# A quarter of the side turns of block 0 go to batch 2, and the last weights are queued behind the evictions

## The chip, the cores and the metric

The kernel runs on one core of one Trainium2 chip. A core has a matrix engine (TensorE, PE in the profile), a vector engine (VectorE, DVE), an activation engine (ScalarE, ACT), a general engine (GpSimd, POOL) and SyncE (SP), which here issues all transfers. Each has its own instruction queue and works through it in order; semaphores tie them together. The metric is the device time of one execution in microseconds.

## The reference

Three networks in a row, on 8 batches of 576 tokens, 512 channels:

```python
# 1 attention: softmax of q over channels, of k over tokens
kv = einsum('bhsd,bhse->bhde', k_s, v);  x = einsum('bhsd,bhde->bhse', q_s, kv)
# 2 Fourier mixing and an MLP
u  = x + real(fft(fft(x, axis=1), axis=2))
un = (u - mean(u)) / sqrt(var(u) + 1e-6)
x  = u + maximum(un @ w_ch1, 0) @ w_ch2            # 512 -> 2048 -> 512
# 3 channel mixing with the token before
xk = mu_k * x + (1 - mu_k) * x_prev;  xr = mu_r * x + (1 - mu_r) * x_prev
k  = maximum(xk @ w_k, 0)                          # 512 -> 1024
out = sigmoid(xr @ w_r) * ((k * k) @ w_v)
```

## The kernel before

The 4608 tokens are cut into nine blocks of 512 (`blocks`, 0 to 8), which don't coincide with the eight batches (0 to 7): block 1 holds tokens of batches 0 and 1, block 2 of 1 and 2, and so on. Each float32 product is made of three float16 products (high by high, high by low, low by high), so that every weight has to be split into two float16 halves on the chip first.

**The main loop** (lines 966 to 1023) is network 2's MLP, block by block. For each of 16 column groups f, `mm1(f)` issues 12 matmuls into a PSUM bank `h` (two buffers), which ACT (`hh`, line 988) and DVE (`hl`, line 989) evict into two float16 halves; this pair is called the eviction here. `mm2(f - 2)` issues 12 matmuls that add the halves of two groups before into four banks `acc`. At the end of a block, line 1021 adds `acc` to `U` on DVE and line 1022 stores it.

**The strands** run beside it. `front_x` is attention, batch after batch, each in two halves (`attention`, lines 318 to 435: a maximum and exponentials of k and q on DVE and ACT, the product `kv`, three groups of transposes, four products into `U`). `front_y` is the Fourier transform of a batch (`transform`) and, for each block whose last batch is done, its normalisation (`norm`); block i + 1 can start only when `norm(i + 1)` and `halves(i + 1)` are done. `front_z` decodes and splits the MLP's weights during block 0. All three are Python generators. Their PSUM tiles in block 0 and later are `side0` and `side1`, one buffer each, taken by turns in the order in which the program asks for them (`aside`, line 64).

`side()` (line 935) gives the strands their turns: it is called 3 times in `mm1(f)` for f below 8 of block 0, twice in any other `mm1`, twice in each `mm2`. While block 0 runs, a call makes eight steps, x and y by turns, until attention of batch 1 is done; then four steps of y alone until `norm(1)` is done (line 939); then x, y, x, y.

**The last strand** (`last_strand`, line 951) gets one step in each call of `side()` once the three fronts are done. Its steps are: 1 of set-up; 40 pieces that take the largest absolute value of network 3's weights (lines 716 and 717); two that turn it into scales; 40 pieces that decode (lines 165 to 168) and 40 that split (lines 755 and 756), by turns; then `load_y(0)`, which reads block 0 back, `bound(0)` (lines 776 to 794), `mix(0, 1)` and `mix(0, 0)` (lines 798 to 828), which make the inputs of network 3 for block 0. If they are not used up when block 8 ends, the loop at line 1024 calls `side()` until they are.

**Network 3** (lines 1028 to 1098): for each block four groups of 12 matmuls with `wr` (line 1046), then eight of `mmk` (line 1059) and eight of `mmv` (line 1074). Line 1046 of block 0 reads what `mix(0, 1)` made, line 1059 what `mix(0, 0)` made.

The order in each engine's queue isn't the program's. A scheduler at build time runs through the program with a timeline of its own, and puts next on each engine the earliest traced instruction that is ready then, so a piece of a strand can stand far ahead of its place in the program. Where an order is wanted, `mark(name, ...)` remembers instructions, and `with behind(name):` lets every instruction traced under it on the same engine come after them (lines 308 to 316).

Of the kernel before, what the change touches and what calls it, by code (L numbers as in the profile page):

```python
# [13 lines left out]
AF = mybir.ActivationFunctionType  # L14
ALU = mybir.AluOpType
# [28 lines left out]
def net(ctx, tc, q, k, v, w1, w2, mu_k, mu_r, w_k, w_v, w_r, ce_d, se_d, cs_d, ss_d, alt_d, id_d, out):  # L44
    nc = tc.nc
# [13 lines left out]
    def bank(tag, bufs, shape=(128, 512)):  # L59
        return ps.tile(list(shape), F32, tag=tag, name=tag, bufs=bufs)  # L60
# [17 lines left out]
    def segments(i):  # L78

        t0, n = blocks[i]  # L80
        done, found = 0, []
        while done < n:
            b, s = divmod(t0 + done, S)
            m = min(n - done, S - s)
            found.append((b, s, m, done))
            done += m
        return found
# [179 lines left out]
    def w1t(t, f):  # L267

        k = place[0, 4 * (f // 4) + t]
        o = 128 * (f % 4)  # L270
        return wf[:, k, o:o + 128], wf[:, k, 512 + o:640 + o]

    def w2t(f, x):
        k = place[1, f]
        o = 128 * x
        return wf[:, k, o:o + 128], wf[:, k, 512 + o:640 + o]
# [31 lines left out]
    def mark(name, *ins):  # L308
        marks[name] = ins

    def behind(name):

        es = ExitStack()
        for i in marks.get(name, ()):
            es.enter_context(tc.issue_after(i.ins))
        return es
# [127 lines left out]
    done_att = [-1]  # L444
# [115 lines left out]
    done_norm = [-1]  # L560
# [115 lines left out]
    def halves(i):  # L676

        halves_part(i, 0, blocks[i][1])
# [178 lines left out]
    def front_x():  # L857
        for b in range(B):
            yield from attention(b)
        front_left[0] -= 1  # L860

    def front_y():
        for b in range(B):
            yield from transform(b)
            for i in range(NB):
                if segments(i)[-1][0] == b:
                    yield from norm(i)
        front_left[0] -= 1

    def front_z():  # L870
        for c in range(17):
            if c < 16:
                decoded(0, c)
            if c > 0:
                squares(0, c - 1)
            yield 0
        scales(0)
        for c in range(16):
            largest(c)
            yield 0  # L880
        scales(1)
        for c in range(4):
            split(0, c)
            yield 0
        for c in range(4):
            decoded(1, c)
            yield 0
        for c in range(2):
            split(1, c)
            yield 0  # L890
        started[0] = True
        have[:] = 4, 2
        for c in range(2, NF):
            if c + 2 < NF:
                decoded(1, c + 2)
            split(1, c)
            have[1] += 1
            yield 0
            if c < NF - 2:
                split(0, c + 2)  # L900
                have[0] += (c + 2) % 4 // 3 * 4
            yield 0
        front_left[0] -= 1
        stage.close()
        W["fx"] = front.enter_context(tc.tile_pool(name="fx", bufs=1))
# [4 lines left out]
    def run(g):  # L910
        for _ in g:
            pass

    def step(g):

        return next(g, None)

    nc.scalar.preload_act_table_set("natural_log_exp_and_others")
    sx, sy, sz = front_x(), front_y(), front_z()
# [13 lines left out]
    late = [None]  # L933

    def side():

        if done_block[0] < 0:

            turns = (sx, sy) * 4 if done_att[0] < 1 else (sy,) * 4 if done_norm[0] < 1 else (sx, sy) * 2
        else:  # L940
            turns = (sx, sy) * (2 if done_block[0] < 3 else 1)
        for g in turns:
            with behind(BEHIND_X.get(half[0]) if g is sx else None):
                step(g)
        if front_left[0] == 0:
            if late[0] is None:
                front.close()
                late[0] = last_strand()
            step(late[0])

    def last_strand():
        yield from last_weights()
        while done_block[0] < NB - 2:
            yield -1
        load_y(0)
        yield 0
        yield from mix(0, 1)
        yield from mix(0, 0)
        if NB > 1:
            load_y(1)  # L960
        late_done[0] = True
# [4 lines left out]
    for i, (t0, n) in enumerate(blocks):  # L966
        acc = [bank(f"acc{x}", 1) for x in range(4)]
        H = {}

        def mm1(f):  # L970
            if i == 0:

                while have[0] < min(f + AHEAD, NF):
                    assert step(sz) is not None
            xh, xl = un[i]
            pt = bank("h", 2)

            m = 256 if i == 0 and f < 8 else n
            for o in range(0, n, m):
                for t in range(4):  # L980
                    wh, wl = w1t(t, f)
                    for z, (a, c) in enumerate(((wh, xh), (wh, xl), (wl, xh))):
                        mm(out=pt[:, o:o + m], lhsT=a, rhs=c[:, t, o:o + m], start=(t == z == 0), stop=(t == 3 and z == 2))  # L983
                    if t == 1:
                        side()
            hh = hq.tile([128, 512], F16, tag="hh", name="hh", bufs=3)
            hl = hq.tile([128, 512], F16, tag="hl", name="hl", bufs=3)
            nc.scalar.activation(out=hh[:, 0:n], in_=pt[:, 0:n], func=AF.Relu)  # L988
            nc.vector.scalar_tensor_tensor(out=hl[:, 0:n], in0=pt[:, 0:n], scalar=0.0, in1=hh[:, 0:n], op0=ALU.max, op1=ALU.subtract)  # L989
            H[f] = hh, hl  # L990
            side()

        def mm2(f):
            if i == 0:
                while have[1] < min(f + AHEAD, NF):
                    assert step(sz) is not None
                if f == NF - LAG:
                    run(sz)
            hh, hl = H.pop(f)
            for x in range(4):  # L1000
                wh, wl = w2t(f, x)
                for z, (a, c) in enumerate(((wh, hh), (wh, hl), (wl, hh))):
                    mm(out=acc[x][:, 0:n], lhsT=a, rhs=c[:, 0:n], start=(f == z == 0), stop=(f == NF - 1 and z == 2))  # L1003
                if x == 1:
                    side()
            side()

        for f in range(NF):
            mm1(f)
            if f >= LAG:  # L1010
                mm2(f - LAG)
        if i + 1 < NB:
            while done_norm[0] < i + 1:
                side()
            halves(i + 1)
        for f in range(NF - LAG, NF):
            mm2(f)
        for x in range(4):
            for b, s, m, o in segments(i):
                y = U[b][:, x, s:s + m]  # L1020
                nc.vector.scalar_tensor_tensor(out=y, in0=acc[x][:, o:o + m], scalar=wsc[:, 6:7], in1=y, op0=ALU.mult, op1=ALU.add)
                nc.sync.dma_start(out=yT[x, :, t0 + o:t0 + o + m], in_=y)
        done_block[0] = i
# [10 lines left out]
    for i, (t0, n) in enumerate(blocks):  # L1034
# [7 lines left out]
        for x, (o, m) in enumerate(subs):  # L1042
            pt = bank("h", 2)
# [167 lines left out]
```

## Time and profile before

| | us |
|---|---|
| median of three runs | 1581.63 (1581.33 to 1582.81) |
| profiled execution | 1582.21 |
| its span in the profile | 1580.4 |
| PE busy in the span | 1465.5 (93%) |
| DVE busy | 938.1 (59%) |
| ACT busy | 652.0 (41%) |
| POOL busy | 245.0 (16%) |

The stages on the span's clock: attention and transform of batch 0 until 103, block 0 from 106 to 247, block 1 from 259.75, block 2 from 382.04, block 3 from 508.84, block 7 from 927.4 to 1021, block 8 from 1021.7 to 1104.8, network 3 from 1104.83. A busy PE isn't idle, but it can run at the lower of two clocks; the granted clock of a stretch (1.00 is 2.4 GHz, 0.50 is 1.2 GHz) tells. Idle time of an engine other than PE costs nothing by itself.

### The profile page before, as it was taken

Reading aid. Unit: us, or ns where it says so; the run is one execution under the profiler, and the core shown is the slowest. Engines: PE = TensorE matmul, PEld = TensorE weight load, DVE = VectorE, ACT = ScalarE, POOL = GpSimd, SP = SyncE. Lnnn points to the kernel's source line nnn. Section 1 sums busy time; section 2 is a strip of 40 time slices with the busy share of each in tenths; the row PEclk is TensorE's granted clock in tenths of the full one; section 3 lists DMA queues with packets and bytes.
Section 4 is the critical chain, followed back from the end, with each engine's and each line's share of the span. In section 5 each row is a group of like instructions: output and inputs, shape, how many; then the busy total and the mean of one; then the engine's idle time right before and its main releaser. Section 6 shows DMA issues by size and latency. Waiting matters only on the chain.

```text
span 1580.4 us, 18510 instructions
## 1 busy us (share of the span) xinstructions
PE 1465.5 (93%) x7135; PEld 765.2 (48%) x7135; DVE 938.1 (59%) x1646; ACT 652.0 (41%) x1167; POOL 245.0 (16%) x183
## 2 busy tenths in 40 slices
PE   5547998997998999999999998999999999999999
PEld 4434654554554555555555443444444444444444
DVE  7789726647658665474452778551785456554423
ACT  5675523423334332333321555241665445544322
POOL 1525522002002020010100236200000000000000
PEclk8769998998998999999999999999999999999999
DMA  8665103202112101101001834100111011100000
GB/s 308 211 205 177 48 1 103 64 1 74 48 47 74 48 33 43 48 32 42 1 7 47 288 117 145 40 26 14 67 54 51 4 54 54 54 0 27 27 27 27
DMA packets 46292, 108.20 MB, mean 68 GB/s; under 512 B 5979, under 2 KB 12412, under 8 KB 46204
## 3 DMA queue, kind: packets, MB, share of 16 engines
q1 hardware_dynamic: 46204, 107.02, 19.8%
q8 instruction: 56, 0.92, 0.2%
q14 instruction: 32, 0.26, 0.1%
HBM read 88.12 MB, written 18.87 MB: 68 GB/s over the span
## 4 chain that ended last, share of the span: by engine, by line
PE 71%; DVE 16%; ACT 4%; DMA 3%; issue 2%; POOL 2%; SPq 0%; POOLq 0%; ACTq 0%; DVEq 0%
PE h L983 18%; PE acc L1003 18%; PE h L1059 12%; PE acc L1074 9%; PE h L1046 4%; PE side L508 2%; PE side L528 2%; PE side L376 1%; DVE aa L820 1%; PE side L429 1%; DMA raw<-in_w_dram 1%; DVE wr L215 1%; DVE eo L463 1%; DVE d L657 1%; DVE wr L214 1%
## 5 line engine op out<-in xcount | busy, mean ns | idle before, releaser
L983 PE MATMUL h<-unh,wr 128*128 128x512 f16 (+1 forms) x1216 | 378.7, 375 | 23.3 <-DVE hl L989 14.0
L1003 PE MATMUL acc<-hh,wr 128*128 128x512 f16 x1152 | 367.6, 380 | 3.2 <-ACT wr L264 2.0
L983 PEld LDWEIGHTS <-wr 128*128 128x128 f16 x1824 | 177.3, 99 | 224.4 <-issue 36.9
L1003 PEld LDWEIGHTS <-wr 128*128 128x128 f16 x1728 | 165.2, 98 | 194.8 <-issue 5.9
L983 PE MATMUL h<-unl,wr 128*128 128x512 f16 (+1 forms) x608 | 226.6, 373 | 4.5 <-DVE unl L671 4.5
L1003 PE MATMUL acc<-hl,wr 128*128 128x512 f16 x576 | 219.6, 381 | 0.0
L989 DVE SCALAR_TENSOR_TENSOR hl<-h,hh 128x512 f16<-128x512 f32 x144 | 99.0, 688 | 187.0 <-ACT hh L988 186.2
L1074 PE MATMUL acc<-wvh,kke 128*128 128x512 f16 x576 | 181.3, 379 | 0.0
L1059 PE MATMUL h<-x,wkh 128*128 128x512 f16 x576 | 171.3, 379 | 0.0
L988 ACT ACTIVATE hh<-h 128x512 f16<-128x512 f32 x144 | 85.1, 592 | 187.8 <-PE h L983 187.4
L1074 PEld LDWEIGHTS <-kke 128*128 128x128 f16 x864 | 84.5, 98 | 102.0
L1064 ACT ACTIVATE kke<-kke 128x512 f32<-128x512 f32 x72 | 45.1, 626 | 166.7 <-DVE kke L1063 163.0
L1063 DVE SCALAR_TENSOR_TENSOR kke<-h,rg 128x512 f32<-128x512 f32 x72 | 49.6, 689 | 102.6 <-PE h L1059 102.3
L1074 PE MATMUL acc<-wvl,kke 128*128 128x512 f16 x288 | 109.2, 379 | 0.0
L1059 PE MATMUL h<-x,wkl 128*128 128x512 f16 x288 | 109.1, 379 | 0.0
L1046 PE MATMUL h<-wrh,x 128*128 128x512 f16 x288 | 88.6, 379 | 1.5 <-ACT kke L1047 1.5
L1059 PEld LDWEIGHTS <-wkh 128*128 128x128 f16 x576 | 55.7, 98 | 65.8
L1066 DVE TENSOR_TENSOR kke<-kke 128x512 f16<-128x512 f32 x72 | 49.7, 690 | 60.7 <-ACT kke L1065 60.3
L1046 PEld LDWEIGHTS <-x 128*128 128x128 f16 x432 | 42.3, 98 | 53.3 <-issue 3.0
L605 POOL TENSOR_TENSOR sq<-u 128x128 f32<-128x128 f32 (+7 forms) x15 | 23.8, 1588 | 281.4 <-DVE u L550 142.7
L826 POOL TENSOR_TENSOR s<-s 128x1024 f32<-128x1024 f32 x9 | 21.2, 2351 | 284.6 <-ACT s L824 234.2
L820 DVE SCALAR_TENSOR_TENSOR aa<-y,ms,aa 128x512 f32<-128x512 f32 x72 | 61.8, 866 | 5.0 <-ACT aa L816 3.0
(335 smaller groups left out, 2232.5 us busy)
## 6 DMA issues: line engine op xcount, KB each, us to landing
raw<-in_w_dram SPq DMA_DIRECT2D x24, 512.0 KB, 4.4
words<-in_w_dram SPq DMA_DIRECT2D x24, 512.0 KB, 4.3
vt<-in_v_dram SPq DMA_DIRECT2D x16, 650.0 KB, 5.1
kt<-in_k_dram SPq DMA_DIRECT2D x16, 576.0 KB, 3.9
qt<-in_q_dram SPq DMA_DIRECT2D x16, 576.0 KB, 3.7
out_dram<-oo SPq DMA_DIRECT2D x36, 256.0 KB, 2.1
y<-yT SPq DMA_DIRECT2D x8, 1026.0 KB, 4.9
raw<-in_w_k_dram SPq DMA_DIRECT2D x32, 256.0 KB, 3.9
```

Of the source, the lines that this page charges most:

```text
L508: mm(out=pt, lhsT=a[:, e, g, js], rhs=c[:, g, :], start=first, stop=(e == 1 and g == 1 and a is el))
L820: nc.vector.scalar_tensor_tensor(out=a, in0=y[:, t, 1:n + 1], scalar=mu[:, w, 0, t:t + 1], in1=a, op0=ALU.mult, op1=ALU.add)
L983: mm(out=pt[:, o:o + m], lhsT=a, rhs=c[:, t, o:o + m], start=(t == z == 0), stop=(t == 3 and z == 2))
L988: nc.scalar.activation(out=hh[:, 0:n], in_=pt[:, 0:n], func=AF.Relu)
L989: nc.vector.scalar_tensor_tensor(out=hl[:, 0:n], in0=pt[:, 0:n], scalar=0.0, in1=hh[:, 0:n], op0=ALU.max, op1=ALU.subtract)
L1003: mm(out=acc[x][:, 0:n], lhsT=a, rhs=c[:, 0:n], start=(f == z == 0), stop=(f == NF - 1 and z == 2))
L1046: mm(out=pt[0:m, :], lhsT=a[:, t, o:o + m], rhs=c[:, t, :], start=(t == 0 and a is rh and c is wrh), stop=(t == 3 and a is rl))
L1059: mm(out=pt[:, 0:n], lhsT=a[:, t, fs], rhs=c[:, t, 0:n], start=(t == 0 and a is wkh and c is kh), stop=(t == 3 and a is wkl))
L1063: nc.vector.scalar_tensor_tensor(out=kr[:, 0:n], in0=pt[:, 0:n], scalar=0.0, in1=G[:, 0:n], op0=ALU.max, op1=ALU.mult)
L1064: nc.scalar.activation(out=kr[:, 0:n], in_=kr[:, 0:n], func=AF.Square, scale=2.0 ** -76)
L1066: nc.vector.tensor_tensor(out=l2[:, 0:n], in0=kr[:, 0:n], in1=h2[:, 0:n], op=ALU.subtract)
L1074: mm(out=acc[x][0:m, :], lhsT=a[:, o:o + m], rhs=c[:, f, :], start=(f == 0 and a is h2 and c is wvh), stop=(f == NFK - 1 and a is l2))
```

## The change

Of the four steps in a call of `side()` in block 0, between the end of batch 1's attention and the end of `norm(1)`, the third goes to x. And each step of the last strand is traced behind the latest eviction that was traced before it: its ACT instructions after that `hh`, its DVE instructions after that `hl`. PE, POOL and SP instructions of the step are not held.

```diff
@@ side()
-            turns = (sx, sy) * 4 if done_att[0] < 1 else (sy,) * 4 if done_norm[0] < 1 else (sx, sy) * 2
+            turns = (sx, sy) * 4 if done_att[0] < 1 else (sy, sy, sx, sy) if done_norm[0] < 1 else (sx, sy) * 2
@@
             if late[0] is None:
                 front.close()
                 late[0] = last_strand()
-            step(late[0])
+            with behind("out"):
+                step(late[0])
@@ mm1(f)
-            nc.scalar.activation(out=hh[:, 0:n], in_=pt[:, 0:n], func=AF.Relu)
-            nc.vector.scalar_tensor_tensor(out=hl[:, 0:n], in0=pt[:, 0:n], scalar=0.0, in1=hh[:, 0:n], op0=ALU.max, op1=ALU.subtract)
+            ma = nc.scalar.activation(out=hh[:, 0:n], in_=pt[:, 0:n], func=AF.Relu)
+            mv = nc.vector.scalar_tensor_tensor(out=hl[:, 0:n], in0=pt[:, 0:n], scalar=0.0, in1=hh[:, 0:n], op0=ALU.max, op1=ALU.subtract)
+            mark("out", ma, mv)
             H[f] = hh, hl
             side()
```

## Rows read from the trace of the kernel before

**Rows 1.** Busy time by stretch: from:to, length, five engines (instructions), granted clock, DMA share, GB/s

```profile
247.00:262.00 15.00, 8.23 (x24) 4.51 (x23) 9.59 (x15) 7.25 (x13) 5.38 (x3) 0.66 0.43 141
360.00:390.00 30.00, 21.22 (x98) 11.40 (x97) 22.46 (x36) 10.48 (x16) 9.03 (x6) 0.83 0.29 97
490.00:515.00 25.00, 17.75 (x70) 10.84 (x69) 24.80 (x38) 10.73 (x20) 3.87 (x3) 0.73 0.27 98
...
927.00:1021.50 94.50, 86.86 (x390) 38.60 (x389) 69.69 (x157) 43.75 (x93) 42.47 (x38) 0.98 0.28 89
1021.50:1104.80 83.30, 83.30 (x388) 37.95 (x387) 29.50 (x59) 22.73 (x37) 2.34 (x1) 1.00 0.07 26
909.60:913.50 3.90, 3.83 (x10) 1.37 (x10) 3.87 (x17) 3.69 (x10) 0.74 (x1) 0.56 0.75 254
```

**Rows 2.** PE's waits, 880 to 924, then 955 to 1002: sum, times, longest

```profile
PE h L983 <- DVE hl L989: 3.8, 2, 3.0
...
PE h L983 <- DVE hl L989: 7.6, 5, 2.7
```

**Rows 3.** Timeline in block 7: start, length, engine, line, operation [idle before, releaser]

```profile
977.81 0.57 ACT L988 ACTIVATE hh<-h 128x512 f16<-128x512 f32 x1
...
978.37 0.95 DVE L756 SCALAR_TENSOR_TENSOR wvl<-dec,pw,wvh 128x256 f16<-128x256 f32 x1
...
979.58 0.68 DVE L989 SCALAR_TENSOR_TENSOR hl<-h,hh 128x512 f16<-128x512 f32 x1
...
980.31 0.38 PE L983 MATMUL h<-unh,wr 128*128 128x512 f16 x1 [2.74 <-DVE hl L989]
```

**Rows 4.** Groups by line: pieces of the last strand on DVE (busy us, mean ns)

```profile
L756 DVE SCALAR_TENSOR_TENSOR wvl<-dec,pw,wvh 128x256 f16<-128x256 f32 x16 | 8.8, 564 | 3.5 <-ACT wvh L755 3.5
...
L167 DVE SCALAR_TENSOR_TENSOR dec<-raw,dec 128x256 uint32<-128x256 uint32 x40 | 16.9, 433 | 0.0
...
L166 DVE TENSOR_SCALAR dec<-raw 128x256 uint32<-128x256 uint32 x40 | 15.1, 377 | 0.1
```

**Rows 5.** Timeline: bound and mix of block 0, last eviction, start of network 3

```profile
869.34 2.26 DVE L781 TENSOR_REDUCE z<-y 128x1 f32<-128x2052 f32 x1
...
1027.33 0.29 DVE L689 TENSOR_REDUCE z<-side 128x1 f32<-128x128 f32 x1 [1.49 <-PE side L688]
...
1029.23 1.33 ACT L816 ACTIVATE aa<-y,ms 128x512 f32<-128x512 f32 x2 [1.53 <-DVE ms L791]
...
1038.67 0.68 DVE L822 TENSOR_TENSOR x<-aa,x 128x512 f16<-128x512 f32 x1
...
1097.89 0.69 DVE L989 SCALAR_TENSOR_TENSOR hl<-h,hh 128x512 f16<-128x512 f32 x1 [4.49 <-ACT hh L988]
1103.30 2.73 DVE L1021 SCALAR_TENSOR_TENSOR u<-acc,wsc,u 128x512 f32<-128x512 f32 x4 [4.72 <-PE acc L1003]
...
1104.83 0.38 PE L1046 MATMUL h<-wrh,x 128*128 128x512 f16 x1
...
1115.73 0.59 PE L1059 MATMUL h<-x,wkh 128*128 128x512 f16 x2
```

**Rows 6.** Timeline: side banks in block 0, then the starts of blocks 1 and 2

```profile
196.26 0.47 PE L508 MATMUL side<-seh,eh 128*128 128x256 f32 x1
...
202.85 0.47 PE L508 MATMUL side<-seh,eh 128*128 128x256 f32 x1
...
244.20 1.06 PE L376 MATMUL side<-vt,kt 128*128 128x130 f32 x8
...
250.70 1.89 DVE L336 TENSOR_REDUCE m<-kt 128x256 f32<-128x1024 f32 x1 [0.69 <-DMA kt<-in_k_dram]
...
259.75 1.06 PE L983 MATMUL h<-unh,wr 128*128 128x512 f16 x2
...
269.50 1.16 PE L376 MATMUL side<-vt,kt 128*128 128x130 f32 x8
...
382.04 1.01 PE L983 MATMUL h<-unh,wr 128*128 128x512 f16 x2 [0.30 <-ACT unh L670]
```

## The prediction

> **What bounds the kernel now.** I read the engine shares first: PE is busy 93% of the span, so only its idle time and its time at the lower clock can be won. Then busy time by stretch, to see where these lie, since a share over the whole span hides it. Three places belong to the first edit: the ends of blocks 0, 1 and 2, where PE idles 6.8, 8.8 and 7.3 us and the granted clock of the stretch is 0.66, 0.83 and 0.73 [rows 1]. One belongs to the second: blocks 6 and 7, where PE's list of waits has seven on `hl`, 3.8 and 7.6 us in sum [rows 2]. Block 8, beside which DVE is busy 29.5 of 83.3 us, loses nothing [rows 1]: it is the cover that the second edit has to use.
>
> Third, the timeline at one such wait [rows 3]. `mm1` starts at 980.31, 0.05 us after the `hl` of the group just before it ends (979.58 + 0.68). So although `h` has two buffers, the schedule takes again the one freed last, and the next `mm1` waits for the newest eviction. Its cover is one `mm2`, 12 matmuls or 2.6 us. `hh` (0.57) and `hl` (0.68) fit in that if they go at once, with some 1.3 us to spare; here a split piece of 0.95 us and a decode stand between them [rows 3].
>
> **Second edit, what it wins.** The pieces were moved by the scheduler to before the evictions that precede them in the program. Held behind, at most the four pieces of one group stand between two evictions. By the groups by line a split costs DVE 0.56 us, a decode 0.38 + 0.43 [rows 4]; two of each, which is the program's rate, make 2.7 us, with `hl` 3.4, in a group of 5.2 us (83.3 / 16 in block 8 [rows 1]). They can start as soon as `hl` is done, so the next eviction finds its queue empty. Won: 3.8 + 7.6 = 11.4 us of waiting, and the clock that dropped after two of the waits: the stretch behind the 3.0 us wait runs at 0.56 for 3.9 us with PE busy, which loses 1.7, twice 3.4 [rows 1, 2]. Together 14.8 us. I keep 1.0 back for stray waits: 13.8. Lower bound: only block 6 is cleared, since no piece can run in it any more (3.8 + 1.7 = 5.5); upper 14.8.
>
> **Second edit, what it costs.** Every step of the last strand is held, not only the weights. Count the turns. `norm(8)` waits for `halves(7)` at the end of block 6; four of its 11 steps fit in the four calls left there, so the fronts end in the eighth call of block 7, and the strand gets 57 of that block's 64 calls. Block 8 gives 64 more: 121. But the weights take 1 + 40 + 2 + 80 = 123 steps. So two splits, `load_y(0)`, `bound(0)`, `mix(0, 1)` and `mix(0, 0)` are traced after block 8, behind its last eviction. Now they run far ahead: the reduction of `bound(0)` at 869.34, the mixes from 1029.23, `mix(0, 1)` done at 1039.35 [rows 5], hidden by block 8. After the change none of it starts before that eviction ends at 1098.58, and the first matmul of network 3, at 1104.83 now, needs it [rows 5]. The transfer of `load_y(0)` goes by SP and isn't held. Queued behind the held instructions is nothing but network 3 itself; the `acc` additions at 1103.30 (2.73 us for four) are ready in the midst and go first [rows 5].
>
> DVE's queue from 1098.58: the pieces of the last seven calls and the two after them, six splits and three decodes, 6 x 0.56 + 3 x 0.81 = 5.8; the additions 2.73; the reduction 2.26 [rows 4, 5]. That is 1109.4. Then the maximum over partitions through PE and the small scales: from 1027.33 to 1029.23, less an `hl` of 0.69 that ran in it, 1.2 [rows 5]; with the product before them, some 2: 1111.4. Four tiles of `mix(0, 1)`: from 1029.23 to 1039.35 is 10.1, less the reduction of another block (2.26) and two `hl` (1.4): 6.5 [rows 5]. So the last tile is there at 1117.9. The four tiles arrive 1.6 us apart and the first of the four `wr` groups takes them as they come, so it ends at 1118 where it now ends at 1107.4 (a group takes 2.6 us; the four fill the time from 1104.83 to 1115.73, bar 0.5 of smaller products [rows 5]): 10.6 us late. The next three groups, 7.8 us, cover `mix(0, 0)`, so that little is added there. PE stands idle for several us before it: after the idle time at the ends of blocks 0 to 2 the clock was granted at its lower level for part of the stretch [rows 1], so I add 1 us. Cost 11.6. Bounds: if the pieces are done while PE is still in block 8, the chain is the PE product at 1104.83 itself (everything of block 8 goes first on PE, which is why the present one waits until 1027), + 2 + 6.5, so 1113.3 and 6 us late; if the additions, splits and both mixes lie one behind the other with a slow stretch, 17. I take 11.6, near the middle, since it is the sum of the queue.
>
> Second edit: -13.8 + 11.6 = **-2.2** us (from -8.8 to +11.5).
>
> **A rule that speaks against this.** The waits repeat at each group. The Trainium skill, Perfetto Trace Analysis, section Optimization Strategy, says that the same gap repeating on the engine that should be saturated can mean that PSUM is too short for the next tile. By it the bank, not the queue, would be the cause, and the waits of block 7 would come again with any pieces beside it; the sum would be -5.5 + 11.6 = +6.1. The rows bear out the half of it, that the newest bank is waited for.
>
> **First edit.** Batch 2's first half now asks for its banks after all 13 of batch 1's transform and norm: its `kv` runs at 244.20 [rows 6], in the last us of block 0. After the change eight steps of it lie between theirs: `kv` and two transposes among the transform's, the third transposes and two products among the norm's. In that stretch one bank comes round in 6.6 us (196.26 to 202.85), so two banks take a tile each 3.3 us [rows 6]. Three more tiles ahead of the transform's end put `norm(1)` back by up to 9.9 us, at least by their PE time, 3.4; the other tiles lie in the norm's own pauses. I take 6.6, the middle. Back come 2.6: at 250.00 the norm's next step stood behind a reduction of batch 2's second k, which waited for a transfer that starts only after `kv` and then took 1.89 [rows 6]; that load now lands 40 us sooner. Block 1 starts at 259.75 + 6.6 - 2.6 = 263.8, 4 us late.
>
> What it gives back: batch 2's second half has its exponentials done by then, so its `kv` comes right after the first half's products, some two bank rounds after the norm's last mean, near 262.5 instead of 269.50 [rows 6]: 7 us earlier, and with it transform 2 and `norm(2)`. Block 2's start, 382.04 now [rows 6], could be 375; PE alone allows 263.8 + 122.3 - 8.8 - 2 (idle and slow time of that end) = 375.3. So 6.7 us earlier at block 2. Half of that I expect to be lost again at the ends of blocks 1 and 2, where the same strands meet with new partners and 8.8 and 7.3 us of idle time show how easily one stands behind the other: **-3.4** us. Bounds: +9 (the late start isn't given back, and its slow clock comes on top), -9 (all of it and two more of block 2's end).
>
> Marks and `with` cost nothing: they add no instruction. No PE, DVE or ACT work is added or removed, and the SBUF tiles stay.
>
> **Sum** against the profiled execution: 1582.2 - 2.2 - 3.4 = 1576.6; the profile lies 0.6 above the median of the runs, so 1576.0.
>
> **The rivals.**
> *Network 3's start costs more than the waits* (slower). At 1104.83, where the mixes are no longer hidden: 17 us and more with the slow stretch, against 14.8; with nothing from block 0's edit, 1584 to 1592, I put it at 1587. It decides once the first `wr` group ends 15 us late, after 1122. For it: eight dependent steps on two engines, all counted at their bare lengths. Against: the queue's sum is 10.6. 0.20.
> *The interleaving only delays block 1* (slower): 9 us late at 259.75, block 2 no earlier, 1581.6 + 9 - 2.2 = 1588. For it: three tiles are put into a chain that block 1 waits for. Against: PE idles at two later ends for the same strands. 0.08.
> *The waits come again* in block 7: the newest bank stays the one that is waited for, and any piece between `hh` and `hl` still holds it; -5.5 + 11.6 - 3.4 on 1581.6, 1584, within the bound or just past it. 0.10. That is what the page's rule above would give.
> *The hold doesn't reach the mixes*, or they start early enough: 14 us won, 6 or less paid, 1581.6 - 8 - 3.4 = 1570, down to 1564. 0.12. For it: only two steps too many push them out of block 8; against: the count is of the program, and no mix can be traced before the 124th step.
> *Both edits cancel* to 1580 to 1583. 0.08.
>
> **How the numbers follow.** The forecast, 1572 to 1578 around 1576, has the other 0.42. About 0.2%, or 3.2 us, is what a measurement here can tell from no change: 1578.5 to 1584.8. Faster: 0.42 less a little at its rim, and 0.12: 0.53. Slower: 0.20 + 0.08, less 0.01: 0.27. The same: 0.20. The forecast's own range is 1572 to 1580. The range of 8 in 10 takes in the cheap start and most of the slower cases: 1566 to 1589.
>
> **What would show it.** Right: no `hl` among PE's waits of blocks 6 to 8; pieces beside block 8 until 1097; line 816 of block 0 after 1098, PE idle 5 to 10 us before line 1046, which now waits for line 821 or 822; `kv` of batch 2 near 204, block 1 late by 2 to 8 us, block 2 early. Wrong: mixes still at 1030, `hl` waits in block 8, or block 2 starting late.

## The result, and the profile after

The changed kernel takes 1590.41 us (median; 1589.34 to 1593.44) where the kernel before took 1581.48 beside it (1579.23 to 1582.81): ratio 1.0061, 95% interval 1.0043 to 1.0079. It is slower by 8.9 us, and 1576.0 was forecast. The profiled execution spans 1589.0 us after 1580.4.

I begin with busy time by stretch, as in [rows 1], around the place of the second edit. The columns are from:to, length, busy time of PE, PEld, DVE, ACT and POOL (instructions), PE's granted clock, DMA share, GB/s. The kernel after, from the last us of block 5 to the first groups of network 3:

```profile
829.00:928.00 99.00, 99.00 (x475) 48.73 (x474) 37.54 (x58) 22.32 (x39) 11.41 (x8) 1.00 0.13 44
928.00:1018.00 90.00, 90.00 (x417) 40.78 (x415) 53.89 (x163) 36.03 (x83) 10.15 (x10) 1.00 0.50 159
1018.00:1090.00 72.00, 72.00 (x335) 32.57 (x334) 45.35 (x102) 29.16 (x72) 22.21 (x29) 1.00 0.30 95
1090.00:1160.00 70.00, 59.84 (x258) 26.16 (x257) 57.11 (x120) 44.03 (x77) 7.66 (x6) 0.90 0.17 61
```

PE is busy without a gap from block 6 to the end of block 8, at the full level; the waits of [rows 2] and the slow stretch behind them are gone. From 829.0 to the end of block 8 the kernel before needed 275.8 us (to 1104.83 [rows 5]); after it is 260.0 (836.62 to 1096.65), so 15.8 less. Then network 3 begins with 10.2 us of idle time. PE's waits there, sum, times, longest:

```profile
PE h L1048 <- ACT x L821: 6.9, 1, 6.9
PE h L1048 <- ACT kke L1049: 1.7, 1, 1.7
PE side L688 <- DVE rg L838: 0.8, 1, 0.8
PE h L1061 <- DVE kke L1065: 0.6, 1, 0.6
PE side L848 <- ACT rb L840: 0.2, 1, 0.2
```

The timeline of the same place (start, length, engine, line, operation, idle before and releaser; lines after 983 stand one or two further down than before), the answer to [rows 5]:

```profile
1090.14 2.28 DVE L781 TENSOR_REDUCE z<-y 128x1 f32<-128x2052 f32 x1
...
1096.27 0.38 PE L688 MATMUL side<-dg,onesr 128*128 128x128 f32 x2
...
1101.25 1.33 ACT L816 ACTIVATE aa<-y,ms 128x512 f32<-128x512 f32 x2 [3.11 <-DVE ms L791]
...
1103.60 0.61 PE L1048 MATMUL h<-wrh,x 128*128 128x512 f16 x1 [6.95 <-ACT x L821]
...
1107.29 2.28 DVE L781 TENSOR_REDUCE z<-y 128x1 f32<-128x2052 f32 x1
1109.49 0.68 DVE L822 TENSOR_TENSOR x<-aa,x 128x512 f16<-128x512 f32 x1
...
1118.77 0.59 PE L1061 MATMUL h<-x,wkh 128*128 128x512 f16 x2
```

The mix starts at 1101.25 where it started at 1029.23. Seen from block 8's last matmul, the first `mmk` comes 22.1 us later (1096.65 to 1118.77); before it was 10.9 (1104.83 to 1115.73). That is 11.2 late. From there to the end of the span it is another 5.5 (470.2 us after, 464.7 before): the waits of 0.8, 0.6 and 0.2 us in the list fall at 1125 to 1127, one more drop of the clock follows them, and a mix is late once more at 1181 (0.8 us). The start of network 3 thus pays 16.8 and takes the 15.8 back.

The rest comes from the ends of blocks 0 to 2. The kernel before and, below it, the kernel after, same columns; the last three rows of each are the stretches there in which the granted clock was at its lower level:

```profile
220.00:300.00 80.00, 72.27 (x354) 39.92 (x353) 49.49 (x85) 27.13 (x46) 13.43 (x8) 0.94 0.22 72
360.00:420.00 60.00, 51.22 (x258) 28.58 (x256) 45.58 (x70) 21.30 (x37) 10.45 (x8) 0.91 0.24 80
480.00:540.00 60.00, 52.75 (x265) 31.63 (x263) 49.87 (x74) 24.68 (x41) 8.90 (x6) 0.89 0.20 70
540.00:645.00 105.00, 102.17 (x519) 55.35 (x519) 56.81 (x85) 32.57 (x60) 10.50 (x7) 1.00 0.10 34
251.30:261.50 10.20, 6.71 (x17) 4.03 (x18) 6.55 (x9) 4.96 (x10) 4.65 (x2) 0.50 0.29 99
377.60:387.80 10.20, 6.12 (x16) 3.13 (x17) 7.90 (x9) 2.95 (x7) 6.06 (x3) 0.50 0.32 106
500.50:514.10 13.60, 10.79 (x34) 7.47 (x35) 13.52 (x21) 7.47 (x15) 2.23 (x1) 0.50 0.23 79
```

```profile
220.00:300.00 80.00, 66.90 (x315) 36.40 (x314) 49.45 (x79) 25.53 (x44) 13.61 (x8) 0.87 0.16 56
360.00:420.00 60.00, 56.19 (x277) 29.48 (x276) 41.67 (x64) 19.89 (x34) 10.68 (x8) 0.94 0.21 70
480.00:540.00 60.00, 47.41 (x226) 28.61 (x225) 46.47 (x66) 23.64 (x43) 9.78 (x7) 0.83 0.16 57
540.00:645.00 105.00, 103.72 (x535) 57.15 (x534) 67.72 (x100) 35.08 (x63) 11.98 (x8) 1.00 0.14 46
252.80:273.30 20.50, 10.89 (x26) 4.61 (x27) 11.71 (x14) 6.06 (x9) 6.49 (x4) 0.50 0.00 2
382.50:389.40 6.90, 5.90 (x15) 2.02 (x14) 6.89 (x13) 1.31 (x3) 1.80 (x2) 0.51 0.43 110
502.00:522.50 20.50, 12.30 (x40) 8.61 (x41) 20.30 (x30) 10.19 (x18) 2.79 (x2) 0.50 0.12 38
```

PE's idle time in the first four stretches is 26.6 us before and 30.8 after: 5.4 more ahead of block 1, 5.0 less ahead of block 2, 5.3 more ahead of block 3, 1.5 less ahead of block 4. Busy time at the lower level counts too: PE is busy there for 23.6 us before and 29.1 after, and half of it is lost, 11.8 and 14.5. So 4.2 idle and 2.7 slow, 6.9 together. Block 4 starts 9.3 late, or 9.7 from the first `mm1`, but not all of that is loss: 13 products of a transform that stood behind its start now stand ahead of it. Block 5 starts 7.5 late (734.3 after 726.8) and block 6 7.6 (836.6 after 829.0). With the 15.8 won and the 16.8 paid that makes the 8.6 by which the span grew. The starts, read off PE's timeline (first `mm1` of each block; "first" is the first `mm1` of block 0, since a run is up to 2 us early or late there):

| kernel | first | block 1 | block 2 | block 3 | block 4 | median, us | ratio to before |
|---|---|---|---|---|---|---|---|
| before | 106.1 | 259.8 | 382.0 | 508.8 | 620.6 | 1581.5 | 1 |
| after | 105.7 | 266.5 | 381.3 | 516.2 | 629.9 | 1590.4 | 1.0061 |
| pieces held, `e3` | 104.8 | 258.4 | 379.9 | 507.2 | 619.0 | 1566.1 | 0.9899 |
| pieces held, turns, `e4` | 104.8 | 265.2 | 380.9 | 516.6 | 631.6 | 1573.4 | 0.9949 |
| `e4`, maximum on POOL, `e5` | 102.9 | 261.7 | 369.6 | 506.9 | 620.0 | 1565.8 | 0.9907 |
| `e3`, maximum on POOL, `e6` | 106.6 | 267.6 | 385.3 | 528.1 | 641.2 | 1584.7 | 1.0020 |
| `e4`, halves held, `e9` | 104.8 | 266.3 | 403.6 | 524.1 | 632.4 | 1575.9 | 0.9975 |
| `e3`, turns in the norm, `e12` | 102.7 | 253.1 | 373.6 | 506.0 | 616.4 | 1565.9 | 0.9912 |

Why nothing came early: the kernel after, PE's timeline for batch 2, against [rows 6] (with the ACT step, line 670, that makes block 1's first input):

```profile
203.56 1.06 PE L376 MATMUL side<-vt,kt 128*128 128x130 f32 x8
...
260.56 0.69 PE L344 MATMUL side<-ident,m 128*128 128x128 f32 x2 [0.50 <-ACT u L430]
262.31 1.15 ACT L670 ACTIVATE unh<-d 128x512 f16<-128x512 f32 x2 [1.81 <-POOL d L657]
265.50 1.22 PE L348 MATMUL side<-ident,wsc 128*128 128x128 f32 x4 [4.26 <-DVE wsc L346]
...
266.51 1.06 PE L984 MATMUL h<-unh,wr 128*128 128x512 f16 x2
...
273.52 1.06 PE L376 MATMUL side<-vt,kt 128*128 128x130 f32 x8
```

The first half's `kv` moved from 244.20 to 203.56, as forecast. The second half's came at 273.52 and not at 262.5: line 344, the maximum of its k over the partitions, asks for a side bank itself, in order behind the first half's products, and runs at 260.56. The exponential of k and `kv` wait for that maximum. Its second product, line 348, besides stands in PE's queue right ahead of block 1's first `mm1` and waits 4.26 us for DVE; in the kernel before it stood behind the first matmuls of block 1, at 264.92. The kernel before makes block 1's first input here:

```profile
258.38 1.14 ACT L670 ACTIVATE unh<-d 128x512 f16<-128x512 f32 x2
```

After, it comes 3.9 us late (262.31), and block 1's first `mm1` 6.8 late: the rest is the wait at line 348.

### The profile page after: what moved, and what is told of

Same layout as the page of the kernel before. It is cut to its first block, busy times and chain, and to the rows that moved or that the text cites. A ratio compares the mean times of both kernels' runs of the same rounds, so it can differ in the third digit from the quotient of the medians.

```text
span 1589.0 us, 18522 instructions
## 1 busy us (share of the span) xinstructions
PE 1467.2 (92%) x7135; PEld 763.1 (48%) x7135; DVE 947.2 (60%) x1646; ACT 646.1 (41%) x1167; POOL 236.4 (15%) x183
## 4 chain that ended last, share of the span: by engine, by line
PE 72%; DVE 17%; ACT 5%; DMA 3%; issue 2%; POOL 1%; SPq 0%; ACTq 0%; DVEq 0%; POOLq 0%
PE h L984 21%; PE acc L1005 19%; PE h L1061 11%; PE acc L1076 8%; PE h L1048 3%; DVE aa L820 2%; PE side L508 2%; PE side L528 2%; PE side L376 1%; PE side L429 1%; DVE eo L463 1%; DVE x L822 1%; DMA qt<-in_q_dram 1%; DVE wr L215 1%; ACT aa L816 1%
## 5 line engine op out<-in xcount | busy, mean ns | idle before, releaser
L1048 PE MATMUL h<-wrh,x 128*128 128x512 f16 x288 | 90.6, 387 | 10.2 <-ACT x L821 6.9
L821 ACT ACTIVATE x<-aa 128x512 f16<-128x512 f32 x72 | 43.9, 623 | 42.0 <-PE h L1061 19.0
```

The source lines that it names most:

```text
L821: nc.scalar.activation(out=h[:, t, 0:n], in_=a, func=AF.Copy)
L1048: mm(out=pt[0:m, :], lhsT=a[:, t, o:o + m], rhs=c[:, t, :], start=(t == 0 and a is rh and c is wrh), stop=(t == 3 and a is rl))
```

## The experiments

Each kernel is the kernel before with the edit shown. All were timed beside the kernel before.

**One edit at a time.** `e1` has only the turns:

```diff
-            turns = (sx, sy) * 4 if done_att[0] < 1 else (sy,) * 4 if done_norm[0] < 1 else (sx, sy) * 2
+            turns = (sx, sy) * 4 if done_att[0] < 1 else (sy, sy, sx, sy) if done_norm[0] < 1 else (sx, sy) * 2
```

> The first edit alone: the four turns beside block 0 are y, y, x, y; nothing is held. Theory (the two edits add up, and the first one only delays): block 1 starts near 266.5 where it started at 259.75, block 2 near 381 as before, block 3 near 516 where it started at 508.84, and from there about 7.5 us late up to block 6; blocks 6 and 7 then keep their waits on hl of some 11 us, so the time is 1581.5 + 7.6 = 1589. Rival (the delay of 7.6 us is taken up by block 7 and the start of network 3, whose work is far ahead without the hold, so that the turns cost nothing at the end): 1580 to 1583. Rival 2 (it was the hold that made block 3 late): 1576 to 1579, as forecast.

1590.89, ratio 1.0059 (1.0039 to 1.0078): +9.4 us, blocks 1 and 3 starting at 265.3 and 514.8. The turns alone make the loss. `e2` has only the hold, marks included:

```diff
-                step(late[0])
+                with behind("out"):
+                    step(late[0])
```

> The second edit alone: every step of the last strand is put behind the evictions traced before it; the turns are as in the kernel before. Theory: blocks 6 and 7 lose their waits on hl and the slow clock behind two of them, some 16 us; the start of network 3 pays some 17, since the bound and both mixes of block 0 are traced after block 8 and stand behind its last eviction. Sum near +1: 1581 to 1584. Rival (the win in blocks 6 and 7 came from the strands' later position, hence from the first edit): 1592 to 1598, with hl waits left in block 7. Rival 2 (the forecast's own sum, start 11.6): 1577 to 1580.

1580.47, ratio 0.9991 (0.9980 to 1.0001): -1.0 us, not to be told from no change. Its waits beside blocks 6 to 8 are none, and at network 3 they are nearly those of the kernel after (6.4 and 1.8 us on line 1048, where that has 6.9 and 1.7).

So the hold's gain doesn't depend on the turns. -1.0 and +9.4 add up to +8.4 of the 8.9 measured.

**The hold without its price.** `e3` and `e4` hold the 123 steps of the weights and leave the load, the bound and the mixes free; `e4` has the turns as well.

```diff
+    steps = [0]
...
+            steps[0] += done_block[0] >= 0
-                step(late[0])
+                with behind("out" if steps[0] <= 123 else None):
+                    step(late[0])
```

> The hold on the 123 steps of the last weights alone; the load, the bound and the mixes of block 0 are free, as in the kernel before; the turns are as before. Theory (the start of network 3 pays because those steps are held): line 816 of block 0 runs inside block 8 again, the first product of network 3 follows block 8 without a gap of over 1 us, and the time is 1581.5 - 14 to 16: 1566 to 1568. Rival (the start is late because the last splits stand behind the last evictions, held or not, and the mixes behind them in the queue): mixes after 1085, the start 6 us or more late, 1572 to 1576. Rival 2 (the freed steps come between the evictions of block 8 and the waits on hl come again there): hl waits of some 5 to 10 us in block 8, 1573 to 1580.

1566.05, ratio 0.9899 (0.9880 to 0.9918): -15.5 us, with no wait of PE at all between 829 and 1180. Its mix and its start of network 3 (line 816 on ACT, lines 1050 and 1063 on PE, the first product and the first `mmk`):

```profile
1013.08 1.33 ACT L816 ACTIVATE aa<-y,ms 128x512 f32<-128x512 f32 x2 [2.12 <-DVE ms L791]
...
1087.30 0.38 PE L1050 MATMUL h<-wrh,x 128*128 128x512 f16 x1
...
1098.20 0.59 PE L1063 MATMUL h<-x,wkh 128*128 128x512 f16 x2
```

The mix runs at 1013, and the first `mmk` follows the first product by 10.9 us, as before the change. The hold on the pieces wins 15.5; holding the bound and the mixes as well costs 1580.5 - 1566.1 = 14.4.

> Both edits, but only the 123 steps of the last weights are held; the load, the bound and the mixes of block 0 are free. Theory (the edits add up): the time of the run with the hold on the weights alone plus the 7.6 us of the turns, 1573 to 1576, with block 3 starting near 516. Rival (the lateness of block 3 is taken up later once nothing holds the mixes): within 2 us of that run, 1566 to 1569.

1573.35, ratio 0.9949 (0.9931 to 0.9966). The turns cost 7.3 here, 9.4 alone and 9.9 on top of the full hold: the same within what the medians scatter.

`e7` asks whether being held or being traced late is what costs. It holds every step, but takes two of them in each call beside block 8, so that the mixes are traced inside it.

```diff
-                step(late[0])
+            for _ in range(2 if done_block[0] == NB - 2 else 1):
+                with behind("out"):
+                    step(late[0])
```

> Every step of the last strand is held, as in the second edit, but beside block 8 each call takes two steps of it, so that the load, the bound and the mixes of block 0 are traced inside block 8 and not after it; the turns are as before. Theory (the start of network 3 pays 14.4 us because these steps are traced after block 8, behind its last eviction; being held costs nothing in itself): line 816 of block 0 well before block 8's end, no wait of over 1 us ahead of network 3, the time of the run with the hold on the weights alone, 1565 to 1568. Rival (held mixes wait for each eviction in turn and come late anyway, or pieces twice as dense beside block 8 bring the waits on hl back): 1570 to 1580.

1568.73, ratio 0.9922 (0.9909 to 0.9934), the mix at 1063 and PE's only waits between 829 and 1180 these:

```profile
PE side L688 <- DVE dg L686: 1.9, 1, 1.9
PE h L985 <- DVE hl L991: 1.2, 2, 0.8
```

Held steps are nearly free if they are traced before the last evictions; it is their place after block 8 that costs. The 3.1 us of waits are about what separates it from `e3`.

**Why the turns lose.** `e5` is `e4` with the maximum of batch 2's second half on POOL, so that it needs no side bank; `e6` is the same on `e3`, without the turns.

```diff
-            if b in MAX_PE:
+            if b in MAX_PE and (b, hf) != (2, 1):
```

> As the run with both edits and the hold on the weights alone (1573.4), but the maximum of batch 2's second half of k over the partitions is taken on POOL instead of through a side bank (in that kernel it waits for a side bank at 259.4, and its kv runs at 272.9). Theory A (the turns bring nothing because this maximum asks for a bank in order, so that batch 2's second half cannot get ahead; the step of the forecast that failed): its kv near 263 to 267, transform 2 some 6 us earlier, blocks 2 and 3 earlier, 1566 to 1569. Rival B (what costs is the late block 1, whose last evictions then lie ahead of batch 3's second half on DVE and ACT; the bank plays no part): the kv earlier or not, block 3 still starting 6 to 8 us late, 1572 to 1575.

1565.78, ratio 0.9907 (0.9890 to 0.9924), 0.0042 under `e4`. The second half's `kv` runs at 257.0. Counted from the first `mm1`, block 2 starts 9.4 us sooner than in `e4`, block 3 7.8 and block 4 9.7: the maximum on PE was what kept batch 2 back, theory A, and without it the loss of the turns is gone, though block 1 is still 5.2 us later than in `e3`. So a late block 1 isn't enough for the loss, against rival B. Whether it is the maximum's bank or its place in PE's queue ahead of block 1 isn't separated, since the edit takes away both. But against `e3` nothing is won: block 2 starts at 369.6 and not at 379.9, block 3 at 506.9 where `e3` has 507.2, and the time is that of `e3`. The two stretches of `e3`, then those of `e5`:

```profile
360.00:420.00 60.00, 51.95 (x255) 28.29 (x254) 46.08 (x70) 22.43 (x39) 9.20 (x7) 0.91 0.24 80
480.00:540.00 60.00, 53.21 (x264) 31.98 (x262) 49.05 (x74) 24.90 (x42) 8.91 (x6) 0.86 0.20 70
```

```profile
360.00:420.00 60.00, 59.88 (x305) 31.41 (x303) 40.66 (x65) 21.51 (x36) 5.56 (x5) 1.00 0.21 70
480.00:540.00 60.00, 42.20 (x205) 26.21 (x204) 45.07 (x67) 23.53 (x38) 9.28 (x6) 0.74 0.15 52
```

The 8 us of idle time ahead of block 2 are gone, and 11 more stand ahead of block 3, with the clock at 0.74.

> The control to the run before it: the hold on the weights alone (1566.1), the turns as in the kernel before, and the maximum of batch 2's second half on POOL. Theories A and B: within 2 us of 1566, since without the turns that half's kv waits for the norm of block 1 anyway. If the maximum through PE was itself what held block 2: 1558 to 1563.

1584.65, ratio 1.0020 (1.0006 to 1.0034): 18.5 us slower than `e3`, which nobody expected, so it is no clean control. Its POOL timeline:

```profile
255.81 1.08 POOL L351 PARTITION_ALL_REDUCE m<-m  x1 [7.13 <-DVE rs L645]
264.56 4.64 POOL L657 TENSOR_TENSOR d<-d,rs 128x1024 f32<-128x1024 f32 x2 [7.67 <-issue]
```

The maximum now lies between norm 1's sums and its last multiplication, which had its input at 255.25 and starts at 264.56; block 1 is 9.2 late, and block 3 21. In `e5` the turns had put the same maximum at 210.4, where POOL had nothing else to do. Here a late block 1 without any turns is followed by a late block 3; in `e5` one with turns was not.

`e8` and `e12` are `e3` with turns for the attention only once the transform of batch 1 is done. In `e8` they are y, y, x, y:

```diff
+            turns = (sx, sy) * 4 if done_att[0] < 1 else (sy,) * 4 if done_dft[0] < 1 else (sy, sy, sx, sy) if done_norm[0] < 1 else (sx, sy) * 2
```

> The hold on the weights alone; the turns beside block 0 are y, y, y, y until the transform of batch 1 is done, and y, y, x, y only from there to the end of its norm. No tile of batch 2 then stands among the transform's, where the first edit put its kv and two transposes. Theory B (the turns cost because these three tiles put norm 1 and block 1 back by 6.8 us): block 1 starts near 259 to 261 and block 3 near 509, 1564 to 1568. Rival (any turn of the attention ahead of the norm's end puts block 1 or block 3 back): block 1 at 263 or later, 1570 to 1575.

1563.53, ratio 0.9892 (0.9876 to 0.9908). It tells nothing: the norm ends after four attention steps, none of which has a product to move, and every engine's instructions stand in the order of `e3`. What is between 1563.5 and 1566.1 is the scatter of the measurement. `e12` has `(sx, sy) * 2` in place of `(sy, sy, sx, sy)`, which does move the products.

> The hold on the weights alone (1566.1); beside block 0 the turns are y, y, y, y until the transform of batch 1 is done, and x, y, x, y from there to the end of its norm. On PE's queue the kv of batch 2's first half then stands ahead of the norm's first mean, and its three transposed tiles between the two means; none is among the transform's tiles, where the first edit put the kv and two of the transposed. Theory (the price of the turns is the tiles among the transform's; the norm's own pauses take them for nothing): kv near 225 to 232, block 1 at 256 to 260, as without the turns, and the time 1564 to 1568, no faster, since an earlier block 2 has bought nothing in the runs so far. Rival (each tile of batch 2 ahead of the norm's second mean puts block 1 back by its round of a bank, 2.5 to 3.3 us): block 1 at 262 or later, 1570 to 1576.

1565.93, ratio 0.9912 (0.9897 to 0.9926), the time of `e3`. `kv` runs at 227.3 and block 1 starts at 253.1, from the first `mm1` 3.2 us sooner than in `e3`: in the norm's pauses these tiles cost nothing. That leaves the `kv` and the two transposed tiles among the transform's as what put the norm back in the first edit. Block 2 starts 4.2 us sooner and block 4 0.5 sooner, both from the first `mm1`. So either change, these tiles out of the transform or the maximum off PE, brings the time back to that of `e3`: the loss takes both.

`e9` was meant to test the place where the late block 1 seemed to be handed on. In the kernel after, the last transposed tile of batch 3's second half is done at 379.44 + 0.27, but its copy stands behind the halves on ACT and behind halves and additions on DVE:

```profile
382.93 1.15 ACT L670 ACTIVATE unh<-d 128x512 f16<-128x512 f32 x2 [1.16 <-POOL d L657]
383.98 0.26 ACT L403 ACTIVATE qT<-side 128x128 fp32r<-128x128 f32 x1
```

On DVE the rest of it (line 405) runs at 389.11, right behind the additions at 387.55 (1.65 us). Its products run from 390.94; in the kernel before the copy went ahead of the halves, at 380.00, and the products began at 380.66.

```diff
-                nc.scalar.activation(out=dst(qT), in_=src, func=AF.Copy)
+                ma = mv = nc.scalar.activation(out=dst(qT), in_=src, func=AF.Copy)
...
+                mark("turn", ma, mv)
...
-            halves(i + 1)
+            with behind("turn" if i == 1 else None):
+                halves(i + 1)
```

(and the same around block 1's additions)

> As the run with both edits and the hold on the weights alone (1573.4), but the halves of block 2 and block 1's last additions are put behind the copies of the last transposed tile of batch 3's second half traced before them. In that run this tile is transposed at 378 but its copy runs at 383.6 on ACT, behind the halves that wait 5.3 us for POOL, and the rest of it on DVE at 388.75, behind the halves and block 1's eight additions; the four products of that half run at 390 to 403, where they ran at 379 to 388 without the turns. Theory (this order on ACT and DVE, brought about by the late block 1, is what makes block 3 late): the products start near 380, transform 3 near 405 instead of 415, block 3 near 508 instead of 516.6, 1565 to 1568. Rival (the late block 1 leaves no idle time of PE ahead of block 2, so that the products stand between block 2's matmuls and evictions whatever ACT and DVE do first): block 3 after 513, 1570 to 1575.

1575.90, ratio 0.9975 (0.9964 to 0.9986). It doesn't answer its question: the tile traced last before the halves was not batch 3's but batch 4's, so the halves waited for that one and block 2 started at 403.6, 22.7 us later than in `e4`. What it shows instead is worth more: block 4 starts at 632.4, in `e4` at 631.6. A block 2 22.7 us late costs 0.8 us two blocks on. (The block 2 of `e5`, 10.3 us sooner than that of `e3`, brought nothing there either: 620.0 against 619.0.)

`e10` and `e11` try to use the idle time ahead of block 3, on `e5` and `e3`:

```diff
-            turns = (sx, sy) * (2 if done_block[0] < 3 else 1)
+            turns = (sy, sy, sx, sy) if done_block[0] == 1 and done_att[0] >= 3 and done_norm[0] < 3 else (sx, sy) * (2 if done_block[0] < 3 else 1)
```

> As the run with the turns and the maximum on POOL (1565.8; block 2 starts there at 369.6, 10 us earlier than without both, but block 3 at 506.9, no earlier), and beside block 2 the turns are y, y, x, y from the end of batch 3's attention to the end of its norm. Theory (block 3 is bound by transform 3 and norm 3, between whose tiles batch 4's first half takes its share of the two side banks): five to eight tiles of batch 4, 2.5 to 3.3 us each on a bank's round, go behind; block 3 starts 6 to 10 us earlier, near 498 to 501, and 1556 to 1560 follows, if batch 4 is still in time for block 4. Rival (batch 4 is then late for block 4, or the last evictions of batch 3 set block 3): 1564 to 1572.

> The hold on the weights alone with the turns beside block 0 as in the kernel before (1566.1), and y, y, x, y beside block 2 from the end of batch 3's attention to the end of its norm. Theory as in the run before it: block 3 6 to 10 us earlier than its 507.2, near 498 to 501, 1557 to 1561. Rival: block 4 late by as much, 1564 to 1572.

1566.97, ratio 0.9918 (0.9903 to 0.9934), and 1563.87, ratio 0.9899 (0.9883 to 0.9915): no gain, but no test either. In both every engine's instructions stand in the order of `e5` and of `e3`. The two side banks are taken by turns only while block 0 runs; from then on the attention has `side0` and transform and norm have `side1` (`aside`, from line 64). So beside block 2 a turn more or less moves no request for a bank, and the premise of both expectations, tiles of batch 4 in the banks that transform 3 waits for, doesn't hold in this program. Whether transform 3 and norm 3 bind block 3 stays open. As repeats the runs give the scatter: with the same order, block 3 starts at 404.0 and 404.9 from the first `mm1` (`e5`, `e10`), and at 402.4, 403.7 and 403.6 (`e3`, `e8`, `e11`). The 0.5 us of `e12` at block 4 lie within that.

Best of all are `e3`, `e5`, `e8`, `e10`, `e11` and `e12`, about 1% under the kernel before and not to be told from each other. `e3` is the simplest: the second edit with its hold ended at the weights, and no first edit.

## Why the prediction was wrong, step by step

**The hold's gain** was right: 13.8 forecast, 15.5 measured by `e3`. It was the order of DVE's queue: `h` kept its two banks, and the 11.4 us of waits of [rows 2] went to none. The Trainium skill, Perfetto Trace Analysis, section Optimization Strategy, reads a gap that repeats as a possible lack of PSUM. The trace does not agree here. Nor did the waits "repeat at each group", as the prediction has it: there are seven in the 32 groups of blocks 6 and 7 [rows 2].

**The hold's price** was right in kind and too small: the steps left over and the wait ahead of the first `wr` product (line 1046 before, 1048 after) came as forecast. To the first `mmk` it was 11.2 us against 11.6, but that is partly luck. The sum put the reduction of `bound(0)` behind the last pieces and additions, 8.5 us after the last eviction; it ran right behind that eviction, beside block 8 (1090.14), and what it led to waited for PE's product at 1096.27, the path that the prediction had for its lower bound. So the mix began 4.6 us after block 8's last matmul and not 6.6. On the other side its four tiles took 8.9 us and not 6.5 (1101.25 to 1110.17), since the reduction of the next block stood among them on DVE, and 1.7 us of waiting for ACT and a slow stretch came on top. The step that failed is "so that little is added there": no wait stands at the first `mmk`, so `mix(0, 0)` was covered, but ACT and DVE were behind with the next work, and 5.5 us more were lost later, 2.4 of them as waits. Measured in all: 14.4 (`e2` less `e3`), inside the bounds of 6 and 17, and 16.8 in the trace of the kernel after. The second edit's sum, -2.2, came as -1.0.

**The first edit** is where the forecast fell, -3.4 against +7.3 to +9.9. Three steps of it failed.
- "Batch 2's second half has its exponentials done by then", and so its `kv` 7 us earlier. Its maximum takes a side bank in order, which the prediction didn't count among the requests; the `kv` ran at 273.52, 4.0 late. `e5` shows it: with the maximum on POOL the `kv` runs at 257.0 (forecast 262.5), and block 2 is 10 us earlier than in `e3` (forecast 6.7).
- "Half of that I expect to be lost again." Against the order without turns all of it is lost, even where it is won: `e5` and `e12` start block 2 earlier than `e3` and block 4 not. An idle stretch of PE was counted as time to be won. That the side strands need it for the work of the next blocks, and that their pace sets block 4, is my reading of `e5`, `e9` and `e12` together; which of their steps does it, and how block 3 comes to start late in the kernel after, stays open, since `e9` to `e11` did not test what they were meant to.
- The sum had no term for the clock except as a bound ("its slow clock comes on top"). At the ends of blocks 0 to 2 idle time grew by 4.2 us and busy time lost to the lower level by 2.7.

The term "block 1 4 us late" was under-sized as well. Its +6.6 was right: the norm's two means run at 243.43 and 253.76, where they ran at 236.87 and 246.87, 6.6 and 6.9 late. The 2.6 were given back as well, for block 1's first input is 3.9 late; but then the maximum's second product, with its wait of 4.26 us, stood ahead of block 1 in PE's queue, and block 1 is 6.8 late. The rival with the name "the interleaving only delays block 1" is the one that came true, at 1588 and with a chance of 0.08; beside it the price of network 3's start ate nearly the whole gain of the hold (14.4 of 15.5), close to what the rival of 0.20 had. The time, 1590.4, lies above the range's 1589.

## What to carry to other kernels

When a hold is put around a generator, look at what it yields last: here 14.4 of 15.5 us hung on whether the hold ends one step before the work that the next stage waits for. Before counting idle time as a gain, ask whose work runs in it; if the next stages wait for that same work, the idle time can come back one block later (`e5` against `e3`), and a start further on (block 4 here) is what should be forecast. And when a strand is to get ahead, list every request that it makes of a shared, ordered resource, the small reductions too, and look for how long the order is shared: here the banks are taken by turns in block 0 alone.

## What the chip showed that was not expected

On POOL, an ordinary operation behind a `PARTITION_ALL_REDUCE` starts some 7 us after it or later, though its input is there: 7.67 in `e6`, where the input had been ready at 255.25 and the reduction ended at 256.89, and 7.03 in `e1` (368.87 + 1.08 to 376.98), both with no releaser in the trace. The timelines of POOL in all 14 traces hold 213 such pairs, and the shortest gap is 6.68 us (`e5`, ahead of 659.78); from an ordinary operation to a reduction, again 213 pairs, it is 5.63 (`e6`, ahead of 515.91). (The profile's spans on POOL are rough.) In `e6` the norm's last multiplication so came 9.3 us after its input; how the 18.5 us of that run follow from it isn't traced block by block. The Trainium skill, GPSIMD Engine Reference, section Instruction dispatch, tells of a load of some 6 us at the first call of a freshly loaded kernel, with no instruction of its own in the profile; the gaps are of that size, but no run here shows what fills them.
